# Six score blocks per visit to the half-high array tiles, and one pool of six PSUM banks, in a fused attention and MLP kernel

## The chip, the cores and the metric

The kernel runs on one core of one Trainium2 chip. The metric is the device time of one execution in microseconds, of the slowest core, which here is the only one. Each kernel is run several times, beside runs of the kernel before on the same chip. All runs quoted here were classed as fast. A ratio always compares with the kernel before in the same session. Engines are named as in the profile: PE does matrix products, PEld is its weight load, ACT is the scalar engine, DVE the vector engine, POOL the general one, SP the one that issues most of the DMA transposes here. A name with a q behind it (SPq) is that engine's sequencer.

## The reference

```python
# u, v: (8, 3008, 256)   z: (8, 3008, 64)   w_in: (256, 2048)   w_out: (2048, 256)
scores = (1 / 3008) * (z @ z.transpose(0, 2, 1))      # per batch: 3008 x 3008, symmetric
attn   = np.maximum(scores, 0.0) ** 2
x      = u * (attn @ v)                               # 24064 tokens of 256
h      = x @ w_in
out    = (h * np.cos(h)) @ w_out
```

The score matrix is symmetric. The kernel computes it in blocks of 512 x 512, and takes a block below the diagonal as the transpose of the one above it.

## The kernel before

The kernel is a list of pieces of work with a time in "units". Each piece is a few matmuls and what follows them on ACT and DVE. The pieces are sorted by their time, and each engine is given its own in that order. A column of 512 tokens of one batch takes eight units; a batch has six columns. There are five kinds of matmul:

- scores (S): 64 rows deep (`dqk` = 64), so that two run side by side in the upper and the lower half of the array (in the trace they start 3 ns apart, and a pair takes the 216 ns of one);
- attention times v (av): 128 rows, 512 columns;
- the last half block of attention (`av_half`): 64 rows, in two halves of the array;
- h = x w_in: 128 rows, 512 columns;
- y = g w_out: 128 rows, 256 columns.

A visit is an uninterrupted run of 64-row matmuls between 128-row ones. Before the change, a visit is one group of four score blocks, on four of the five banks of the pool `ps_w`. (A bank is here one tile of the program's PSUM pools, into which its matmuls write; it holds one block of 128 x 512.) y has a bank of its own, in which two token blocks are interleaved.

```python
gpool = pool("g", 6)
...
ps_w = psum("ps_w", 5)
ps_acc = psum("ps_acc", NDH)
ps_y = psum("ps_y", 1)
...
def direct(b, c, R):                  # batch 0, columns 0-2: all blocks computed
    return b == 0 and c <= 2          # at once, none waits for a transpose
...
def s_diagonal(b, c, also):
    ...                               # 512, 384, 256 and 128 columns: the upper part only
    for k0 in range(0, K, 2):
        ...                           # Relu on ACT, square on DVE, then, for three of four:
                nc.sync.dma_start_transpose(
                    t[:, k + 1:, k, :],
                    t[:, k, k + 1:, :].rearrange("p s w -> p (s w)"))

def s_group(b, c, R, also=None):
    if R == c and (b, c) > (0, 3):
        return s_diagonal(b, c, also)
    ...                               # four matmuls of 512 columns, Relu, squares
    if R > c and not direct(b, R, c):
        tt = tpool.tile([P, K, K, P], FP16, name="tt")
        turned[(b, c, R)] = tt
        nc.sync.dma_start_transpose(  # the mirrored block, 512 x 512
            tt.rearrange("p s k w -> p (s k) w"),
            t.rearrange("p s k w -> p (s k w)"))
```

A diagonal group (R == c) has three small transposes of its own, except where it is computed whole: in columns 0 to 3 of batch 0.

## Time and profile before

The median of the first three runs was 1257.65 us (1257.07 to 1258.25).

| what | value | read from |
|---|---|---|
| PE busy | 1245.4 of 1255.9 us | first part of the page |
| ACT, DVE busy | 68%, 63% | first part of the page |
| a 512-column matmul, start to start | 215.8 ns | start times of PE's matmuls |
| a 256-column matmul | 109.2 ns | the same |
| a visit of four score blocks | 633 ns: 2 x 216 + 201 | the same |
| PE's waits after 62 us | under 1 us | the same, and the view of waits |

First, the page of the kernel before: its span; busy time, share of the span and instructions for PE, DVE and ACT; the clock that PE was granted in 40 slices, in tenths; and the chain of work that ended last.

```profile
span 1255.9 us, 20306 instructions
...
PE 1245.4 (99%) x7533; PEld 672.0 (54%) x7533; DVE 791.0 (63%) x1389; ACT 853.9 (68%) x1516; POOL 145.8 (12%) x201
...
PEclk9999999999999999999999999999999999999999
...
PE 97%; ACT 1%; DVE 1%; issue 0%; DMA 0%; ACTq 0%
```

PE is the chain. Matmuls overlap in this profile (each lasts 379 ns and starts 216 after the one before), so the busy share alone does not tell how full PE is. Start times do.

Second, the timeline of the kernel before around one visit: start, length, engine, line, operation, operands. L308 is av, L249 scores, L365 y.

```profile
510.50 0.38 PE L308 MATMUL acc<-a,v_2_70 128*128 128x512 f16 x1
...
510.81 0.61 PE L249 MATMUL w<-zT_64 64*128 64x512 f16 x4
...
511.34 0.61 PE L365 MATMUL yp<-w_out_73,g 128*128 128x256 f16 x4
```

From the last av to the first score there are 312 ns where 216 are due, and from the last score (at 511.04) to the first y 308. This is what a visit costs beyond its matmuls: 96 ns going in and 93 coming out, and with the small offsets between the pairs 201 ns for a visit.

### The profile page before, as it was taken

How to read it: one execution, taken by the hardware profiler on the slowest of the kernel's cores; microseconds unless marked ns; L12 is line 12 of the kernel's file. 1: busy time of each engine (PE TensorE's matmuls, PEld its weight loads, DVE VectorE, ACT ScalarE, POOL GpSimd, SP SyncE). 2: the span in 40 equal slices, each digit the busy share in tenths (PEclk: the TensorE clock that was granted, in tenths of full speed). 3: DMA queues.
4: the chain of work that ended last, by engine and by line, in shares of the span. 5: the costliest groups of instructions: out<-in, count | busy, mean ns of one | idle time of the engine just before them, and what ended most of it. 6: DMA issues, size and time to landing. Idle time of an engine off the chain costs nothing.

```text
span 1255.9 us, 20306 instructions
## 1 busy us (share of the span) xinstructions
PE 1245.4 (99%) x7533; PEld 672.0 (54%) x7533; DVE 791.0 (63%) x1389; ACT 853.9 (68%) x1516; POOL 145.8 (12%) x201
## 2 busy tenths in 40 slices
PE   8999999999999999999999999999999999999998
PEld 3355555555555555555555555555555555555556
DVE  7766666666666666666666666666666656666555
ACT  6766776676766767666676666766767767766646
POOL 3311001110011100111001110011100111000000
PEclk9999999999999999999999999999999999999999
DMA  9999467875778956787667975679766797565311
GB/s 166 157 190 133 90 113 115 140 123 93 118 110 140 121 99 116 111 141 114 109 110 109 147 114 106 113 106 147 116 105 113 110 139 126 100 110 102 67 34 43
DMA packets 484179, 144.84 MB, mean 115 GB/s; under 512 B 432368, under 2 KB 484080, under 8 KB 484080
## 3 DMA queue, kind: packets, MB, share of 16 engines
q1 hardware_dynamic: 356448, 88.73, 42.5%
q0 software_dynamic: 100400, 29.77, 23.9%
q10 hardware_dynamic: 27232, 25.06, 7.0%
q8 instruction: 59, 0.97, 0.3%
q14 instruction: 40, 0.33, 0.1%
HBM read 60.29 MB, written 24.64 MB: 68 GB/s over the span
## 4 chain that ended last, share of the span: by engine, by line
PE 97%; ACT 1%; DVE 1%; issue 0%; DMA 0%; ACTq 0%
PE acc L308 37%; PE yp L365 26%; PE w L341 26%; PE w L249 5%; PE w L219 1%; PE acc L282 1%; PE w L365 1%; ACT rt L261 0%; DMA x<-in_z_dram 0%; DVE a L264 0%; DVE g L348 0%; ACT zT_63 L197 0%; DVE x L329 0%; PE w L192 0%; ACT L345 0%
## 5 line engine op out<-in xcount | busy, mean ns | idle before, releaser
L341 PE MATMUL w<-x,w_in_72 128*128 128x512 f16 x1504 | 446.2, 379 | 0.2 <-DVE g L348 0.2
L365 PE MATMUL yp<-w_out_73,g 128*128 128x256 f16 x2944 | 442.3, 273 | 0.4 <-ACT ob L373 0.4
L365 PEld LDWEIGHTS <-g 128*128 128x128 f16 x3008 | 285.2, 98 | 207.5 <-issue 41.5
L261 ACT ACTIVATE rt<-w 128x512 f16<-128x512 f32 x489 | 252.8, 604 | 102.6 <-PE w L249 102.6
L264 DVE TENSOR_TENSOR a<-rt 128x1024 f16<-128x1024 f16 x254 | 174.0, 690 | 154.8 <-ACT rt L261 150.1
L341 PEld LDWEIGHTS <-w_in_72 128*128 128x128 f16 x1504 | 147.0, 98 | 22.3 <-issue 3.4
L90 POOL DMA_DIRECT2D ust_62<-in_u_dram x64 | 45.2, 711 | 372.0 <-PE w L249 371.4
L229 ACT ACTIVATE rt<-w 128x512 f16<-128x512 f32 (+3 forms) x176 | 62.7, 443 | 32.7 <-PE w L219 32.7
L308 PE MATMUL acc<-a,v_2_70 128*128 128x512 f16 x304 | 80.0, 379 | 0.0
L308 PE MATMUL acc<-a,v_2_67 128*128 128x512 f16 x304 | 79.7, 379 | 0.0
L308 PE MATMUL acc<-tt,v_0_68 128*128 128x512 f16 (+1 forms) x288 | 73.6, 373 | 0.0
L90 POOL DMA_DIRECT2D ust_61<-in_u_dram x48 | 36.1, 758 | 306.9 <-PE acc L308 297.3
L329 DVE TENSOR_TENSOR x<-acc,ut 128x64 f16<-128x64 f32 (+7 forms) x178 | 69.6, 431 | 1.3 <-PE acc L308 1.3
L308 PE MATMUL acc<-tt,v_0_65 128*128 128x512 f16 (+1 forms) x264 | 67.4, 373 | 0.0
L230 DVE TENSOR_TENSOR a<-rt 128x512 f16<-128x512 f16 (+3 forms) x176 | 48.2, 322 | 27.7 <-ACT rt L229 27.7
L308 PEld LDWEIGHTS <-v_0_65 128*128 128x128 f16 x384 | 36.6, 98 | 47.3 <-issue 5.9
L308 PEld LDWEIGHTS <-v_1_66 128*128 128x128 f16 x384 | 36.6, 98 | 47.3 <-issue 6.6
L308 PEld LDWEIGHTS <-v_0_68 128*128 128x128 f16 x384 | 36.9, 98 | 45.7 <-issue 3.4
L308 PEld LDWEIGHTS <-v_1_69 128*128 128x128 f16 x384 | 36.9, 98 | 44.9 <-issue 2.6
L308 PE MATMUL acc<-a,v_1_66 128*128 128x512 f16 x224 | 59.3, 379 | 0.8 <-DVE x L329 0.7
L308 PE MATMUL acc<-a,v_1_69 128*128 128x512 f16 x224 | 59.4, 379 | 0.0
L373 ACT ACTIVATE ob<-yp 128x512 f32<-128x512 f32 x92 | 56.0, 608 | 1.2 <-PE yp L365 1.2
(1557 smaller groups left out, 1507.6 us busy)
## 6 DMA issues: line engine op xcount, KB each, us to landing
out_dram<-ob ACTq DMA_DIRECT2D x94, 256.0 KB, 3.5
ust_61<-in_u_dram POOLq DMA_DIRECT2D x48, 128.0 KB, 5.9
ust_62<-in_u_dram POOLq DMA_DIRECT2D x32, 128.0 KB, 3.4
a<-a SPq DMA_TRANSPOSE x132, 3.0
v_0_65<-in_v_dram POOLq DMA_DIRECT2D x4, 512.0 KB, 8.1
v_1_66<-in_v_dram POOLq DMA_DIRECT2D x4, 512.0 KB, 6.2
v_0_68<-in_v_dram POOLq DMA_DIRECT2D x4, 512.0 KB, 8.5
v_1_69<-in_v_dram POOLq DMA_DIRECT2D x4, 512.0 KB, 6.9
```

The lines of the kernel that those rows point to most:

```text
L90: hold(nc.gpsimd.dma_start(dst, src))
L219: chain(nc.tensor.matmul(sps[k][:, k * P:], zt[h, j0 + k, :], zt[h, j0 + k:j0 + K, :].rearrange("p j w -> p (j w)"), start=True, stop=True))
L229: nc.scalar.activation(rt[:, i, k * P:], sps[k][:, k * P:], AF.Relu)
L230: nc.vector.tensor_tensor(t[:, k, k:, :].rearrange("p s w -> p (s w)"), rt[:, i, k * P:], rt[:, i, k * P:], ALU.mult)
L249: chain(nc.tensor.matmul(sps[k], zt[h, R * K + k + 1 - lo, :], zt[h, j0:j0 + K, :].rearrange("p j w -> p (j w)"), start=True, stop=True))
L261: nc.scalar.activation(rt[:, i, :], sps[k0 + i], AF.Relu)
L264: nc.vector.tensor_tensor(tv, rv, rv, ALU.mult)
L308: chain(nc.tensor.matmul(acc[nh][:, 0:wn], vs[b % 2][j // G][:, j % G, nh * P:(nh + 1) * P], a, start=(n == 0), stop=(n == NJ - 2)))
L329: nc.vector.tensor_tensor(x[:, nh, :], acc[nh][:, o:o + n], ut[:, nh, o:o + n], ALU.mult)
L341: chain(nc.tensor.matmul(hp, w_in16[:, k, ft * P:(ft + 1) * P], x[:, k, :], start=(k == 0), stop=(k == NDH - 1)))
L365: chain(nc.tensor.matmul(ys[m][:, ts % YP, :], gs[(m, ft // FG)][:, ft % FG, ts * P:(ts + 1) * P], w_out16[:, ft, :], start=(n % (YP * NFT ...
L373: nc.scalar.activation(ob, ys[m], AF.Copy, bias=0.0, scale=inv_s2)
```

## The change

The intent is fewer visits: six score blocks in each, on all six banks of one pool, which y shares. To free y's bank, y is accumulated one token block at a time. The schedule is laid out in steps of two units (four h tiles and 16 y matmuls, then 12 av with a visit among them). v is kept in a ring of four tiles in place of six, which pays for two more g tiles.

```diff
-    vs = [[kpool.tile([P, G, D], FP16, name=f"v{i}_{g}") for g in range(NG)]
-          for i in range(2)]
+    vring = [kpool.tile([P, G, D], FP16, name=f"v{i}") for i in range(NG + 1)]
+    vs = lambda b, g: vring[(b * NG + g) % (NG + 1)]
...
-    gpool = pool("g", 6)
+    gpool = pool("g", 8)
...
-    ps_w = psum("ps_w", 5)
+    ps_w = psum("ps_w", 6)
     ps_acc = psum("ps_acc", NDH)
-    ps_y = psum("ps_y", 1)
...
-    def s_group(b, c, R, also=None):
-        if R == c and (b, c) > (0, 3):
-            return s_diagonal(b, c, also)
...
+    def s_matmuls(b, c, R, p):                 # a pair: two of a group's four blocks
...
+        diagonal = R == c and not direct(b, c, R)
...
+    def s_visit(pairs, also=None):
+        done = [(pair, s_matmuls(*pair)) for pair in pairs]
         if also is not None:
             also()
+        for pair, banks in done:
+            s_squares(*pair, banks)
...
+    NV = 3                                      # pairs in a visit
...
+        for i in range(0, len(pairs), NV):
+            some = [pr for pr in pairs[i:i + NV] if not direct(*pr[:3])]
+            t = b * span - lead + span * i / len(pairs)
+            if some:
+                scores.append((2 * math.floor(t / 2) + 1.2, some))
...
+                for q, f in enumerate(av_chunks(b, c, [4, 2] * (U // 2))):
+                    at(t + q // 2 * 2 + (1.4 if q % 2 else 1.0), 2, f)
```

`(b, c) > (0, 3)` became `not direct(b, c, R)`. The two differ for one group only, the diagonal one of batch 0, column 3.

More of the change, by code (lines that the diff above doesn't have):

```diff
@@ L117, in load_v @@
     def load_v(b, g):
-        t = vs[b % 2][g]
+        t = vs(b, g)
         n, full, rest = rows(v, b, g)
@@ L208, in direct, with s_squares @@
         return b == 0 and c <= 2
-    def s_diagonal(b, c, also):
+    halves = {}
+    def s_matmuls(b, c, R, p):
         zt = zT[b % 2]
-        t = apool.tile([P, K, K, P], FP16, name="a")
-        sps = [ps_w.tile([P, CW], FP32, name="w") for k in range(K)]
-        for k in (0, 1, 3, 2):
-            lo = 1 if k in (1, 2) else 0
+        banks = {}
+        diagonal = R == c and not direct(b, c, R)
+        for k in ((0, 1), (3, 2) if diagonal else (2, 3))[p]:
+            s0 = k if diagonal else 0
+            lo = 1 if k in ((1, 2) if diagonal else (1, 3)) else 0
             h = slice(lo * dqk, (lo + 1) * dqk)
             j0 = c * K + 1 - lo
+            sp = ps_w.tile([P, CW], FP32, name="w")
             chain(nc.tensor.matmul(
-                sps[k][:, k * P:], zt[h, j0 + k, :],
-                zt[h, j0 + k:j0 + K, :].rearrange("p j w -> p (j w)"),
+                sp[:, s0 * P:], zt[h, R * K + k + 1 - lo, :],
+                zt[h, j0 + s0:j0 + K, :].rearrange("p j w -> p (j w)"),
                 start=True, stop=True))
-        if also is not None:
-            also()
-        for k0 in range(0, K, 2):
-            rt = rpool.tile([P, 2, CW], FP16, name="rt")
+            banks[k] = sp
+        return banks
+    def s_squares(b, c, R, p, banks):
+        if p == 0:
+            halves[(b, c, R)] = apool.tile([P, K, K, P], FP16, name="a")
+        t = halves[(b, c, R)]
+        diagonal = R == c and not direct(b, c, R)
+        rt = rpool.tile([P, 2, CW], FP16, name="rt")
+        if diagonal:
             for i in range(2):
-                k = k0 + i
-                nc.scalar.activation(rt[:, i, k * P:], sps[k][:, k * P:], AF.Relu)
+                k = 2 * p + i
+                nc.scalar.activation(rt[:, i, k * P:], banks[k][:, k * P:], AF.Relu)
                 nc.vector.tensor_tensor(
@@ L236, in s_diagonal @@
                         t[:, k, k + 1:, :].rearrange("p s w -> p (s w)"))
-        fresh[(b, c, c)] = [t[:, k, :, :] for k in range(K)]
-    def s_group(b, c, R, also=None):
-        if R == c and (b, c) > (0, 3):
-            return s_diagonal(b, c, also)
-        zt = zT[b % 2]
-        t = apool.tile([P, K, K, P], FP16, name="a")
-        sps = [ps_w.tile([P, CW], FP32, name="w") for k in range(K)]
-        for k in range(K):
-            lo = k % 2
-            h = slice(lo * dqk, (lo + 1) * dqk)
-            j0 = c * K + 1 - lo
-            chain(nc.tensor.matmul(
-                sps[k], zt[h, R * K + k + 1 - lo, :],
-                zt[h, j0:j0 + K, :].rearrange("p j w -> p (j w)"),
-                start=True, stop=True))
+            if p == 1:
+                fresh[(b, c, R)] = [t[:, k, :, :] for k in range(K)]
@@ new lines, in s_squares @@
+            return
+        for i in range(2):
+            k = 2 * p + i
+            if direct(b, c, R) and (k == 3 or c == R == 0 and i):
+                nc.vector.tensor_scalar_max(rt[:, i, :], banks[k], 0.0)
+            else:
+                nc.scalar.activation(rt[:, i, :], banks[k], AF.Relu)
+        rv = rt.rearrange("p k (s w) -> p k s w", s=K)
+        nc.vector.tensor_tensor(
+            t.rearrange("p s k w -> p k s w")[:, 2 * p:2 * p + 2], rv, rv, ALU.mult)
+        if p == 1:
+            fresh[(b, c, R)] = [t[:, :, k, :] for k in range(K)]
+            if R > c and not direct(b, R, c):
+                tt = tpool.tile([P, K, K, P], FP16, name="tt")
+                turned[(b, c, R)] = tt
+                nc.sync.dma_start_transpose(
+                    tt.rearrange("p s k w -> p (s k) w"),
+                    t.rearrange("p s k w -> p (s k w)"))
@@ L253, in s_group @@
+    def s_visit(pairs, also=None):
+        done = [(pair, s_matmuls(*pair)) for pair in pairs]
         if also is not None:
             also()
-        for k0 in range(0, K, 2):
-            rt = rpool.tile([P, 2, CW], FP16, name="rt")
-            for i in range(2):
-                if direct(b, c, R) and (k0 + i == 3 or c == R == 0 and i):
-                    nc.vector.tensor_scalar_max(rt[:, i, :], sps[k0 + i], 0.0)
-                else:
-                    nc.scalar.activation(rt[:, i, :], sps[k0 + i], AF.Relu)
-            tv = t.rearrange("p s k w -> p k s w")[:, k0:k0 + 2]
-            rv = rt.rearrange("p k (s w) -> p k s w", s=K)
-            nc.vector.tensor_tensor(tv, rv, rv, ALU.mult)
@@ L265, in s_group @@
-        fresh[(b, c, R)] = [t[:, :, k, :] for k in range(K)]
-        if R > c and not direct(b, R, c):
-            tt = tpool.tile([P, K, K, P], FP16, name="tt")
-            turned[(b, c, R)] = tt
-            nc.sync.dma_start_transpose(
-                tt.rearrange("p s k w -> p (s k) w"),
-                t.rearrange("p s k w -> p (s k w)"))
+        for pair, banks in done:
+            s_squares(*pair, banks)
     xs = {}
@@ L283, in av_half, with av_chunks @@
                 accs[(b, c)][nh],
-                vs[b % 2][NG - 1][h, G - 1, nh * P:(nh + 1) * P],
+                vs(b, NG - 1)[h, G - 1, nh * P:(nh + 1) * P],
                 a[h], start=False, stop=False))
-    def av_quanta(b, c):
+    def av_chunks(b, c, sizes):
         w = min(CW, S - c * CW)
-        per = -(-NJ // U)
         order = [(c + i) % NC * K + k for i in range(NC) for k in range(K)]
@@ L298, in moving, with chunk @@
             return w, tt[:, k, 0:w]
-        def quantum(q):
-            if q == 0:
+        def chunk(n0, n1):
+            if n0 == 0:
                 accs[(b, c)] = [ps_acc.tile([P, CW], FP32, name="acc") for nh in range(NDH)]
@@ L304, in quantum @@
             for nh in range(NDH):
-                for n in range(q * per, min(NJ - 1, (q + 1) * per)):
+                for n in range(n0, n1):
                     j = order[n]
@@ L309, in quantum @@
                         acc[nh][:, 0:wn],
-                        vs[b % 2][j // G][:, j % G, nh * P:(nh + 1) * P], a,
+                        vs(b, j // G)[:, j % G, nh * P:(nh + 1) * P], a,
                         start=(n == 0), stop=(n == NJ - 2)))
-            if q == U - 1:
+            if n1 == NJ - 1:
                 finish()
@@ L330, in finish @@
                         x[:, nh, :], acc[nh][:, o:o + n], ut[:, nh, o:o + n], ALU.mult)
-        return [lambda q=q: quantum(q) for q in range(U)]
+        ends = [min(sum(sizes[:i]), NJ - 1) for i in range(len(sizes) + 1)]
+        return [lambda i=i: chunk(ends[i], ends[i + 1]) for i in range(len(sizes))]
     gs = {}
@@ L350, with y_quantum @@
     ys = {}
+    obs = {}
     NTS = TW // P
-    YP = 2
-    def y_quantum(m, q):
-        per = NFT * NTS // (2 * U)
-        for n in range(q * per, (q + 1) * per):
-            ts, ft = n // (YP * NFT) * YP + n % YP, n % (YP * NFT) // YP
-            if n % (YP * NFT) == 0:
-                if m >= NT - 2 and n:
-                    ys[m] = ps_w.tile([P, CW], FP32, name="w").rearrange(
-                        "p (t d) -> p t d", d=D)
-                else:
-                    ys[m] = ps_y.tile([P, YP, D], FP32, name="yp")
-            chain(nc.tensor.matmul(
-                ys[m][:, ts % YP, :],
-                gs[(m, ft // FG)][:, ft % FG, ts * P:(ts + 1) * P],
-                w_out16[:, ft, :],
-                start=(n % (YP * NFT) == 0),
-                stop=(n % (YP * NFT) == YP * NFT - 1)))
-            if (n + 1) % (YP * NFT) == 0:
-                ob = opool.tile([P, YP, D], FP32, name="ob")
-                nc.scalar.activation(ob, ys[m], AF.Copy, bias=0.0, scale=inv_s2)
-                r0 = m * TW + (ts - YP + 1) * P
+    def y_quantum(m, ts, f4):
+        if f4 == 0:
+            ys[m] = ps_w.tile([P, CW], FP32, name="w")
+        for ft in range(f4 * FG, (f4 + 1) * FG):
+            chain(nc.tensor.matmul(
+                ys[m][:, 0:D], gs[(m, f4)][:, ft % FG, ts * P:(ts + 1) * P],
+                w_out16[:, ft, :], start=(ft == 0), stop=(ft == NFT - 1)))
+        if f4 == NFT // FG - 1:
+            if ts % 2 == 0:
+                obs[m] = opool.tile([P, 2, D], FP32, name="ob")
+            i = ts % 2
+            nc.scalar.activation(
+                obs[m][:, i, :], ys[m][:, 0:D], AF.Copy, bias=0.0, scale=inv_s2)
+            i0 = i if m == NT - 1 else 0
+            if i or m == NT - 1:
+                r0 = m * TW + (ts - i + i0) * P
                 nc.scalar.dma_start(
-                    out[r0:r0 + YP * P, :].rearrange("(ts p) d -> p ts d", p=P), ob)
+                    out[r0:r0 + (i + 1 - i0) * P, :].rearrange("(ts p) d -> p ts d", p=P),
+                    obs[m][:, i0:i + 1, :])
     events = []
@@ L388 @@
     lead = 1.75 * U
+    NV = 3
     scores = []
+    when = {}
     for b in range(B):
-        for i, (c, R) in enumerate(groups):
-            if not direct(b, c, R):
-                t = math.floor(b * span - lead + span * i / len(groups))
-                scores.append((t - 0.1 if t % U == U - 1 else t + 0.9, b, c, R))
+        pairs = [(b, c, R, p) for c, R in groups for p in range(2)]
+        for i in range(0, len(pairs), NV):
[3 more added lines that the diff above has]
+                scores.append((2 * math.floor(t / 2) + 1.2, some))
         for c in range(NC):
@@ L398 @@
                 for i in range(NC):
-                    scores.append((c * U + 4 * i / 3 - 3.1, b, c, (c + i) % NC))
+                    R = (c + i) % NC
+                    scores.append((c * U + 4 * i / 3 - 3.1, [(b, c, R, 0), (b, c, R, 1)]))
+    for t, some in scores:
+        for pr in some:
+            when[pr[:3]] = max(t, when.get(pr[:3], t))
     also = {}
@@ L403 @@
             t = b * span + c * U
-            ready = 1.5 + max(ts for ts, bb, cc, R in scores
-                              if (bb, cc, R) == (b, c, NC - 1))
-            room = [sc for sc in scores if max(ready, t + 0.6) < sc[0] < t + U - 1.07]
+            ready = 1.5 + when[(b, c, NC - 1)]
+            first, last = (0.6, 6.93) if direct(b, c, c) else (1.0, 7.3)
+            room = [i for i, sc in enumerate(scores)
+                    if max(ready, t + first) < sc[0] < t + last and i not in also]
             if room:
-                also[min(room)] = lambda b=b, c=c: av_half(b, c)
+                also[min(room, key=lambda i: scores[i][0])] = lambda b=b, c=c: av_half(b, c)
             else:
-                at(t + U - 1.07, 3, lambda b=b, c=c: av_half(b, c))
-            for q, f in enumerate(av_quanta(b, c)):
-                at(t + q + (0.5 if q < U - 1 else -0.05), 2, f)
-    for sc in scores:
-        at(sc[0], 3, lambda sc=sc: s_group(*sc[1:], also=also.get(sc)))
+                at(t + last, 3, lambda b=b, c=c: av_half(b, c))
+            if direct(b, c, c):
+                for q, f in enumerate(av_chunks(b, c, [3] * U)):
+                    at(t + q + (0.5 if q < U - 1 else -0.05), 2, f)
+            else:
+                for q, f in enumerate(av_chunks(b, c, [4, 2] * (U // 2))):
+                    at(t + q // 2 * 2 + (1.4 if q % 2 else 1.0), 2, f)
+    for i, (t, some) in enumerate(scores):
+        at(t, 3, lambda i=i, some=some: s_visit(some, also=also.get(i)))
     for m in range(NT):
         b, i = divmod((m + 1) * TW - 1, S)
-        th = max(20 + m * U, (b * NC + i // CW + 1) * U + 1)
+        th = max(20 + m * U, (b * NC + i // CW + 1) * U + 2)
         for ft in range(NFT):
-            at(th + ft // 2 + (0.3 if ft % 2 else 0.1), 1,
-               lambda m=m, ft=ft: h_quantum(m, ft))
-        for q in range(2 * U):
-            at(th + U - 2 + q // 2 + (0.2 if q % 2 else 0.0), 4,
-               lambda m=m, q=q: y_quantum(m, q))
+            at(th + ft // 4 * 2 + ft % 4 * 0.2, 1, lambda m=m, ft=ft: h_quantum(m, ft))
+        for ts in range(NTS):
+            for f4 in range(NFT // FG):
+                at(th + U + 2 * ts + 0.1 + 0.2 * f4, 4,
+                   lambda m=m, ts=ts, f4=f4: y_quantum(m, ts, f4))
     for b in range(B):
@@ L442 @@
             for g in range(NG):
-                at(t + (0.75 * g - 2.5) * U, 0, lambda b=b, g=g: load_v(b, g))
+                at(t + (-1.5, -0.4, -0.1)[g] * U, 0, lambda b=b, g=g: load_v(b, g))
         for c in range(3 if b == 0 else 0, NC):
```

## The prediction

The sum: 10.2 + 0.15 + 0.7 + 0.3, about 11.4 us off, and 1 us on.

> **What bounds the kernel.** TensorE. The page's first part has PE busy 1245.4 of 1255.9 us, ACT 68%, DVE 63%; the chain of waits that ended last is 97% PE. From the start times of its matmuls, a 512-column one takes 215.8 ns of the array, a 256-column one 109.2, and after the first 62 us PE loses under 1 us to waits. So only work taken off PE's own stream counts. The granted clock is 1.0.
>
> **What a visit costs.** The score matmuls (64 rows, in two tiles of the array) and the half-block matmuls of attention interrupt the 128-row stream. Going in, the gap is 311.6 ns where 215.8 is due; coming out, 308.5. A visit of four score blocks takes 633 ns, two pairs at 216 and 201 of switching; one of two half-block matmuls 418, one pair and 202. [...]
>
> **What the change does.** The instruction order shows the same 7533 matmuls before and after. Runs of 64-row matmuls fall from 172 to 121 (57 of six full blocks, 45 with a diagonal): 51 x 0.201 = 10.2 us, all on the critical path. One more diagonal group is done at its smaller size (0.15 us). y by token block in the common pool lets the last 64 y matmuls start while the last g is made, where PE waits 0.7 us before; the last eviction and store are half as large (0.3 us). Total: about 11.4 us.
>
> **What it adds.** 188 y evictions of 256 columns replace 94 of 512. Start to start on ACT, back to back, a 512-column Relu takes 477 ns, a Sin 569, an eviction of half the size about 290 (estimate, from the 256-column Relu's 263): roughly +10 us of ACT, off the path. A six-block visit fills all six banks. A two-unit period with a visit is 6.9 us of PE (8 h matmuls 1.73, 16 y 1.75, 12 attention 2.59, visit 0.85); ACT needs 6 x 0.477 + 4 x 0.569 + 0.29 = 5.4 us, DVE about 3 x 0.61 + 4 x 0.60 = 4.2, with the x evictions at most 5.8. So each catches up even where two periods in a row have visits (four times a batch). After a visit the next h needs the first bank some 1.2 to 1.6 us after the scores began; Relu gives it back after about 1.0 and the others each 0.48 later, while PE asks for one after 0.44, then each 0.87. That is close where the last attention piece has two matmuls, but should cost 0.1 us or less a time: 1 us in all. The v ring has some 19 us for loads that land in 6 to 9: no cost.
>
> **Prediction.** 1257.65 - 11.4 + 1 = about 1247 us, range 1243.5 to 1252. Faster by over 2%: 1%; within 2%: 97%; slower: 2%.
>
> **What would show it.** In the matmul start times: 121 visits, 849 ns for six blocks, 1065 with a half block, entry and exit still near 96 and 93 ns; waits after 62 us still near 1 us.
>
> **What would make it wrong.** Waits of h, y or the third pair of scores on Relu or g (bank turnaround longer than I think), seen as waits of PE on ACT or DVE all through the batches; v late at batch boundaries; more waiting in the first 100 us, where h runs without y; an extra cost when consecutive y matmuls add into the same 256 columns.

## The result, and the profile after

The changed kernel took 1258.69 us (median of 6, 1255.98 to 1261.33), beside 1257.68 for the kernel before. The ratio is 1.0008, with a 95% interval of 0.9992 to 1.0023: the same. A ratio here is the mean time of one kernel's fast runs over the mean of the other's fast runs of the same rounds, so it is not quite the ratio of the medians. About 11 us were predicted and none came.

The page of the changed kernel, the lines that answer to those of before, and one group of matmuls (its last numbers are the idle time before them and what ended it):

```profile
span 1256.7 us, 20414 instructions
...
PE 1238.2 (99%) x7533; PEld 680.4 (54%) x7533; DVE 782.0 (62%) x1391; ACT 845.6 (67%) x1610; POOL 146.0 (12%) x201
...
PEclk9979999999999999999999999999999999999999
...
PE 96%; DMA 2%; DVE 1%; ACT 0%; SPq 0%; issue 0%; DVEq 0%
...
L310 PE MATMUL acc<-a,v_66 128*128 128x512 f16 x312 | 81.3, 385 | 7.7 <-DMA a<-a 6.4
```

PE is busy 7.2 us less in a span of the same length. One slice of the clock reads 7, DMA has entered the chain with 2%, and one group of av matmuls waited 6.4 us for the DMA that turns a score block inside its own tile (a<-a).

The time can be cut at two matmuls that both kernels have. I use the start of the 97th h matmul (in the first batch) and of the 1441st (near the end of the last).

| us | before | after | difference |
|---|---|---|---|
| start to the 97th h | 125.23 | 134.88 | +9.65 |
| 97th to 1441st h | 1088.76 | 1078.82 | -9.94 |
| 1441st h to the end | 41.94 | 42.96 | +1.02 |

So the gain is there, all through the batches, and the first 135 us give it back. The first and the last row also hold a shift of order: before the 97th h the kernel before has done 148 y matmuls and the changed one 128, and the other 20 (2.2 us) come after the 1441st h instead. For the same y work, the start lost 11.8 us and the end gained 1.2.

The steady part is as predicted. Between the two matmuls there are 143 visits before and 96 after, and they take 93.8 and 83.2 us. The timeline of the changed kernel around a visit (L223 is scores):

```profile
633.77 1.89 PE L310 MATMUL acc<-a,v_67 128*128 128x512 f16 x8
635.59 0.82 PE L223 MATMUL w<-zT_63 64*128 64x512 f16 x6
636.34 0.60 PE L310 MATMUL acc<-a,v_67 128*128 128x512 f16 x2
```

From the last of the eight av to the next av there are 850 ns beyond its own 216: three pairs at 216 and again 201 for the visit itself.

The loss is here, in the timeline of PE in the changed kernel (L344 is h, L310 av; the bracket gives idle time and what ended it):

```profile
63.07 3.30 PE L344 MATMUL w<-x,w_in_70 128*128 128x512 f16 x8 [0.75 <-DVE g L351]
66.21 0.38 PE L310 MATMUL acc<-a,v_66 128*128 128x512 f16 x1
71.65 0.59 PE L310 MATMUL acc<-a,v_66 128*128 128x512 f16 x1 [5.06 <-DMA a<-a]
72.92 0.59 PE L310 MATMUL acc<-a,v_66 128*128 128x512 f16 x1 [0.68 <-DMA a<-a]
74.19 2.29 PE L310 MATMUL acc<-a,v_66 128*128 128x512 f16 x5 [0.68 <-DMA a<-a]
```

And this is SP's DMA queue in the same kernel (start, time in the sequencer, what it issues):

```profile
40.92 28.22 SPq L265 DMA_TRANSPOSE tt<-a  x5
69.31 3.74 SPq L245 DMA_TRANSPOSE a<-a  x3
73.10 4.19 SPq L265 DMA_TRANSPOSE tt<-a  x2
```

At 66.21 PE reaches column 3 of batch 0. The first matmul uses the part of the diagonal group that DVE wrote; the next three need the parts that the three small transposes write. DVE had finished the squares at 54.55. The three were issued only at 69.31, 70.58 and 71.86, because five long transposes (128 x 2048 elements each) held SP for 28 us, 5.6 each in the mean (3.7 to 7.6), while the three took 1.2 each. They landed at 71.61, 72.87 and 74.14, and PE went on 0.04 to 0.05 us after each. From the start of the first of these four matmuls to the start of the fourth took 7.98 us, where 0.65 (3 x 216 ns) are due.

In the kernel before, SP had the same long transposes, but nothing of column 3's first matmuls was among them:

```profile
41.13 29.83 SPq L269 DMA_TRANSPOSE tt<-a  x6
71.13 1.76 SPq L150 DMA_TRANSPOSE ut<-ust_62  x1
```

The clock adds to it. In the changed kernel 20 matmuls of 512 columns between 58 and 80 us start some 427 ns apart instead of 216, which is another 4.1 us; the view by windows gives a granted clock of 0.50 from 62.6 to 65.9 us and from 69.4 to 79.6. What makes the clock fall was not shown; what can be read is what came before. Seven of the 20 (1.4 us) begin at 63.07, before the long wait, so that wait did not cause them: they follow 4 us with small waits (1.33, 0.23, 0.23 and 0.75 us), after DVE had stood 4.79 us (to 59.33) for a long transpose. The other 13 (2.7 us) follow the long wait.

### The profile page after: what moved, and what is told of

It is laid out like the page before. It is cut to its first block, busy times and chain, and to the rows that moved or that the text cites. A ratio compares the mean times of both kernels' runs of the same rounds, so it can differ in the third digit from the quotient of the medians.

```text
span 1256.7 us, 20414 instructions
## 1 busy us (share of the span) xinstructions
PE 1238.2 (99%) x7533; PEld 680.4 (54%) x7533; DVE 782.0 (62%) x1391; ACT 845.6 (67%) x1610; POOL 146.0 (12%) x201
## 4 chain that ended last, share of the span: by engine, by line
PE 96%; DMA 2%; DVE 1%; ACT 0%; SPq 0%; issue 0%; DVEq 0%
PE acc L310 37%; PE w L361 26%; PE w L344 26%; PE w L223 6%; DMA tt<-a 1%; PE acc L285 1%; DMA ut<-ust_62 1%; DVE g L351 0%; DMA x<-in_z_dram 0%; SPq L245 0%; DMA a<-a 0%; ACT zT_63 L196 0%; DVE a L258 0%; DVE x L331 0%; ACT rt L256 0%
## 5 line engine op out<-in xcount | busy, mean ns | idle before, releaser
L344 PE MATMUL w<-x,w_in_70 128*128 128x512 f16 x1504 | 447.9, 381 | 0.8 <-DVE g L351 0.8
L361 PE MATMUL w<-w_out_71,g 128*128 128x256 f16 x3008 | 448.6, 273 | 0.0
L361 PEld LDWEIGHTS <-g 128*128 128x128 f16 x3008 | 294.2, 98 | 191.6 <-issue 1.4
L344 PEld LDWEIGHTS <-w_in_70 128*128 128x128 f16 x1504 | 147.6, 98 | 61.1 <-issue 7.3
L310 PEld LDWEIGHTS <-v_66 128*128 128x128 f16 x552 | 52.1, 98 | 68.4 <-issue 21.6
L310 PE MATMUL acc<-a,v_66 128*128 128x512 f16 x312 | 81.3, 385 | 7.7 <-DMA a<-a 6.4
L310 PE MATMUL acc<-a,v_65 128*128 128x512 f16 x336 | 85.8, 380 | 0.0
L310 PEld LDWEIGHTS <-v_67 128*128 128x128 f16 x552 | 52.1, 98 | 59.3 <-issue 12.3
L310 PEld LDWEIGHTS <-v_65 128*128 128x128 f16 x552 | 51.6, 98 | 59.8 <-issue 12.2
L310 PEld LDWEIGHTS <-v_68 128*128 128x128 f16 x552 | 51.9, 98 | 57.7 <-issue 10.9
L310 PE MATMUL acc<-a,v_67 128*128 128x512 f16 x312 | 80.0, 383 | 0.0
L310 PE MATMUL acc<-a,v_68 128*128 128x512 f16 x312 | 79.2, 379 | 0.0
L368 ACT ACTIVATE ob<-w 128x256 f32<-128x256 f32 x188 | 73.0, 388 | 5.3 <-PE w L361 5.3
L310 PE MATMUL acc<-tt,v_68 128*128 128x512 f16 (+1 forms) x240 | 62.2, 371 | 0.0
L310 PE MATMUL acc<-tt,v_67 128*128 128x512 f16 (+1 forms) x240 | 62.1, 371 | 0.0
```

The costliest lines, as they stand in the source:

```text
L310: chain(nc.tensor.matmul(acc[nh][:, 0:wn], vs(b, j // G)[:, j % G, nh * P:(nh + 1) * P], a, start=(n == 0), stop=(n == NJ - 2)))
L344: chain(nc.tensor.matmul(hp, w_in16[:, k, ft * P:(ft + 1) * P], x[:, k, :], start=(k == 0), stop=(k == NDH - 1)))
L361: chain(nc.tensor.matmul(ys[m][:, 0:D], gs[(m, f4)][:, ft % FG, ts * P:(ts + 1) * P], w_out16[:, ft, :], start=(ft == 0), stop=(ft == NFT ...
L368: nc.scalar.activation(obs[m][:, i, :], ys[m][:, 0:D], AF.Copy, bias=0.0, scale=inv_s2)
```

## The experiments

Two theories of the loss stood at this point. Theory A: the diagonal group of batch 0, column 3, now needs transposes that stand behind the long ones. Theory B: the loss comes from what was changed on purpose, that is, visits that fill every bank, bursts of h at the start, and a clock that falls because of them.

### e1: that one group whole again

```diff
-        diagonal = R == c and not direct(b, c, R)
+        diagonal = R == c and (b, c) > (0, 3)
```

(in both places of the changed kernel)

> The changed kernel with one group, the diagonal one of batch 0, column 3, computed whole as in the kernel before (no transposes of its own). Theory A (its three transposes stand behind the long ones in SP's DMA queue, PE waits 5.06 + 0.68 + 0.68 us and then runs 5 us at half clock): about 10 us less than the changed kernel, 1248 us; no wait of PE on a<-a. Theory B (the loss in the first 80 us comes from the longer bursts of h and the six-bank visits, not from this group): 1257 to 1259, the wait moves to another releaser.

Measured: 1248.35 us (median of 6, 1246.67 to 1250.74), ratio to before 0.9915 (0.9895 to 0.9935). That is 10.3 us less than the changed kernel's median; by the ratios to the kernel before (1.0008 and 0.9915) it is 0.93%, or 11.7 us. It was run at another time. The result is correct.

The view of who waited for whom, for PE, in the changed kernel and then in e1 (in us: total, times, longest):

```profile
PE acc L310 <- DMA a<-a: 6.4, 3, 5.1
PE w L223 <- DVE g L351: 3.0, 6, 1.3
PE acc L310 <- DVE x L331: 1.3, 1, 1.3
```

```profile
PE acc L310 <- DVE x L331: 2.9, 1, 2.9
PE w L223 <- ACT zT L196: 1.6, 2, 1.1
PE w L470 <- DVE rt L467: 1.2, 1, 1.2
PE w L223 <- DVE g L351: 1.2, 4, 0.5
```

The wait on a<-a is gone, and column 3 starts at 65.97 us and runs on at full clock, 216 ns from start to start:

```profile
65.97 2.75 PE L310 MATMUL acc<-a,v 128*128 128x512 f16 x12
```

That is only 0.24 us sooner than in the changed kernel, so the half clock before the long wait does not set the two apart. What does is the wait (7.3 us) and the half clock after it (2.7). The 97th h starts at 124.69 us (134.88 in the changed kernel, 125.23 in the kernel before), and the stretch from there to the 1441st is 1078.82 us, the same as in the changed kernel. Theory A holds, and theory B doesn't: the six-bank visits and the bursts of h are all still there.

### e2: the same condition in the kernel before

```diff
-        if R == c and (b, c) > (0, 3):
+        if R == c and not direct(b, c, R):
```

> The kernel before with that one group done as a diagonal one with three transposes, nothing else changed. Theory A: the same stall appears in the kernel before, 6 to 12 us slower than it, 1264 to 1270 us, with PE waiting on a<-a near 60 to 72 us. Theory B: no difference above 1 us.

Measured: 1275.96 us (median of 4), ratio 1.0128 (1.0103 to 1.0152), about 17 us slower than the kernel before. This is more than I had expected. PE gets to column 3 sooner than in the changed kernel (63.77 us against 66.21) and the three transposes are issued later (72.54 against 69.31), so the first wait is 10.75 us against 5.06; and the granted clock is 0.50 from 68 to 84.9 us. The timeline of e2:

```profile
63.77 0.38 PE L308 MATMUL acc<-a,v 128*128 128x512 f16 x1 [0.31 <-DVE x L329]
74.89 0.59 PE L308 MATMUL acc<-a,v 128*128 128x512 f16 x1 [10.75 <-DMA a<-a]
76.15 1.87 PE L308 MATMUL acc<-a,v 128*128 128x512 f16 x4 [0.67 <-DMA a<-a]
```

One condition, for one group, without any of the rest of the change, makes the loss.

### e3: four blocks per visit

```diff
-    NV = 3
+    NV = 2
```

(on top of e1)

> e1 with four score blocks per visit (NV = 2) in place of six: 172 runs of 64-row matmuls in place of 121, everything else as in e1. If a visit's switching costs 0.201 us wherever it stands: e1 + 10.2 us. If the gain of fewer visits is taken by waits on banks (rival): e1 within 3 us.

Measured: 1254.48 us (median of 6, 1252.2 to 1256.53), ratio 0.9963 (0.9941 to 0.9986), so 6.1 us slower than e1. In the steady stretch between the 97th and the 1441st h it takes 1087.00 us, 8.2 more than e1. There it has 143 visits against 96. They take 92.5 us against 83.2, 9.3 more: 0.198 for each of the 47. That is the predicted price. Some 1.1 us come back in the rest of the stretch, which is neither visits nor the nominal time of the other matmuls (1.44 us in e3, 2.58 in e1): e1 has small waits after its fuller visits. The start went 2.4 us better in this profile (97th h at 122.24; the trace has 6.8 us of waits of PE before it, against 8.3 in e1), so the whole kernel shows less than the 10.2 expected. I had expected the total, and it fell between the two theories; the stretch settles it.

### e5: the three transposes from ACT's queue

```diff
-                    nc.sync.dma_start_transpose(
+                    (nc.scalar if b == 0 and c == 3 else nc.sync).dma_start_transpose(
                         t[:, k + 1:, k, :],
```

(on top of the changed kernel)

> The changed kernel with the three transposes of that group issued from ACT's queue, so that they do not stand behind the long ones of SP's queue. If the place in the queue is the cause: they land by about 60 us, no wait of PE on them, about 8 to 10 us less than the changed kernel. If the transposes are slow in themselves under the load of DMA at that time: PE still waits for them for several us, gain under 4 us.

Measured: 1268.96 us (median of 4), ratio 1.008, 10 us slower than the changed kernel. This does not test what it was meant to test. It was run at another time. The view of waits on ACT:

```profile
ACT rt L256 <- DMA a<-a: 20.9, 1, 20.9
```

The first of the three was issued at 75.38, just after the last long transpose of SP had landed at 75.08. In the trace, ACT's sequencer waits before it for eight semaphores, from 57.12 us on. These waits stand in the program as it was built from the edit: the eight semaphores are those of the last eight transposes issued by SP before. (What happens without them was not run.) So the wait did not go away, and it now also stood in front of ACT's Relus. In this run another queue was no way around.

### e6 and e7: the long transposes taken away

To take the queue away without touching the three, the nine long transposes of columns 0 to 2 of batch 0 are replaced by zeros from POOL. The results are wrong (relative error 0.12). e6 is the changed kernel with that edit, e7 is e1 with it.

```diff
                 turned[(b, c, R)] = tt
-                nc.sync.dma_start_transpose(...)
+                if direct(b, c, R):
+                    nc.gpsimd.memset(tt, 0.0)
+                else:
+                    nc.sync.dma_start_transpose(...)
```

> The changed kernel, wrong result on purpose: in batch 0 the nine mirrored blocks of columns 0 to 2 are filled with zeros by POOL in place of the nine long transposes that stand in SP's DMA queue ahead of the diagonal group's three. The three themselves stay. If standing behind the long ones is the cause: they land by about 58 us, no wait of PE on a<-a, and the time is within 2 us of e7_full03_no_queue. If the three are slow by themselves: PE still waits for them and the time is 5 us or more above e7.

> The control to e6: the same zeros (wrong result on purpose), with the group computed whole. It also shows what the nine long transposes cost in all: 1242 to 1247 us, since the waits on u's transposes and on buffers near 40 and 60 us should go too.

Measured: e6 1245.93 us (median of 4, 1243.49 to 1247.21), e7 1244.29 us (1243.63 to 1245.58). They were run at other times. SP's queue and PE in e6:

```profile
20.74 9.50 SPq L150 DMA_TRANSPOSE ut<-ust  x2
53.21 3.74 SPq L245 DMA_TRANSPOSE a<-a  x3
```

```profile
59.52 1.90 PE L347 MATMUL w<-x,w_in 128*128 128x512 f16 x8
61.26 2.75 PE L313 MATMUL acc<-a,v 128*128 128x512 f16 x12
```

The three transposes take the same 3.74 us of the sequencer as in the changed kernel, but at 53.21 in place of 69.31. The last landed at 59.23 (I had expected about 58), and column 3 starts at 61.26 without a wait. Together with the changed kernel and e1 this makes a square (medians):

| | long transposes ahead | none ahead |
|---|---|---|
| three transposes of the group | 1258.69 | 1245.93 |
| group computed whole | 1248.35 | 1244.29 |

With the queue, the three cost 10.3 us; without it, 1.6, which is no more than the scatter of these runs. By the ratios to the kernel before in the same session (1.0008, 0.9915; 0.9888, 0.9878) it is 11.7 us and 1.3. It is their place behind the long transposes, not the three in themselves. The edit also takes the nine transposes out of the DMA's work altogether, so the two columns may differ by more than the queue, but both rows of the second have that alike.

### e8 and e9: two attempts to improve the start

e8 is e1 with a Sin as the first activation, so that ACT loads Sin's table at the beginning. e9 is e8 with u's transposes of columns 1 and 2 placed earlier in SP's queue.

```diff
-        nc.scalar.activation(dummy, pihalf, AF.Relu)
+        nc.scalar.activation(dummy, pihalf, AF.Sin)
```

```diff
-            at(t + c * U + (1 if b or c not in (1, 2) else -3 * c), 0, lambda b=b, c=c: turn_u(b, c))
+            at(t + c * U + (1 if b or c not in (1, 2) else (-6.5, -8)[c - 1]), 0, lambda b=b, c=c: turn_u(b, c))
```

> e1 with the dummy activation at the start a Sin in place of a Relu, so that the table that Sin needs is loaded at 1 us and not at 52 us, where 1.28 us of it stood in front of the first Sin while PE waited 1.5 us on banks: 1 to 1.5 us less than e1, about 1247; no second table load in the trace. If a Relu makes the first table be loaded again, no gain.

> e8 with u's transposes of columns 1 and 2 of batch 0 placed ahead of the long ones in SP's queue: the wait of PE near 39 us (1.4 us in the changed kernel's trace, 3.0 in e1's) goes: 1.5 to 3 us less than e8, about 1244 to 1245. If the long transposes only move the wait to later: within 1 us of e8.

Measured: e8 1249.41 us (median of 6, 1248.11 to 1253.47), e9 1248.28 us (1244.03 to 1254.75). They were run on another chip. Neither differs from e1 beyond the scatter, and e9's 1.1 us below e8 doesn't tell its two expectations apart. In e8 the second table load of 1.28 us (at 52.30 in e1) is gone and the one at 1.28 us is left, and the waits of PE's scores between 50 and 57 us fell from 0.95 us to 0.35 (by the idle times of the timeline), but the wait for u near 39 us was longer in that profile (3.7 us against 3.0), so nothing shows in the total. In e9 the wait for u's transpose went, but DVE then waited for a buffer that a long transpose was still reading, and PE still waited near 40 us. The timeline of e9:

```profile
39.16 1.29 DVE L258 TENSOR_TENSOR a<-rt 128x1024 f16<-128x1024 f16 x2 [1.56 <-DMA tt<-a]
...
41.11 1.24 PE L310 MATMUL acc<-a,v 128*128 128x512 f16 x5 [1.47 <-DVE x L331]
```

e7, which has no long transposes there, is about 4 us below e1 (medians of two sessions): that is what they still cost e1 at the start. What else the start could give was not tried. Whether e8's table load is worth anything by itself stays open; it is below the scatter of the start.

The simplest of the best correct versions is e1, 0.9915 of the time of the kernel before (e9, at 0.9910, does not differ from it).

## Why the prediction was wrong

- "What bounds the kernel" was right. PE is the chain, and what was taken off its stream came off the time, in the steady part.
- "What a visit costs" was right: 633 ns before and 850 after for a visit of four and of six blocks, 201 of it for the visit itself, and about 0.198 us for each visit in e3 against e1.
- "51 x 0.201 = 10.2 us" was right in kind and size. In the measured stretch 47 visits fewer took 10.6 us less. About 1.1 us of that is not switching: seven diagonal visits took 647 ns before, where eight others took 486, and the changed kernel's have the shorter form.
- The 1.0 us for the end (0.7 and 0.3) was near: for the same y work, the stretch after the 1441st h is 1.2 us shorter.
- "1 us in all" for waits on banks was near. What is left of the stretch after the visits and the nominal matmul times (and so holds their rounding too) is 2.58 us after and 1.94 before.
- "The v ring ... no cost" is supported by the trace only: in the changed kernel's view of waits none of PE's, down to 0.4 us, is on a v load. No run changed the ring by itself.
- **The step that failed is "One more diagonal group is done at its smaller size (0.15 us)".** I saw that the condition had changed, counted the array time it saves, and stopped there. A diagonal group also brings three DMA transposes, and column 3 of batch 0 starts with exactly that group. In SP's queue they stood behind five long ones that took 28 us. The term that I put at -0.15 us measured +10.3 (e1 against the changed kernel; 11.7 by the ratios), and +17 in the kernel before (e2).
- The list of what could go wrong named "more waiting in the first 100 us", but for another cause, "where h runs without y". That was not the 10 us: e1 has the same bursts of h. The extra cost it named for consecutive y matmuls that add into the same 256 columns did not come: from one to the next are 109 ns in the changed kernel, as before. But the start of e1 does cost something. It reaches the 97th h 0.5 us before the kernel before does, with 20 y matmuls and 4 visits (3.0 us together) fewer done by then, so it is about 2.5 us behind. Its longest wait is 2.95 us for x at 42.18, which DVE could make only when u's transpose had landed, followed by four matmuls at half clock. This is one profile, and no run separates its causes.

With that one term put right, the prediction stands: e1's 1248.35 us are 1.35 above the 1247 predicted, and inside its range. That it comes so close is in part luck: the 1.1 us of the diagonal visits and the 2.5 us of the start were both not in the sum, and have opposite signs.

## What to carry to other kernels

When a change rewrites a condition, ask for each case that moves from one side to the other what it now waits for, and not only how much work it has. A DMA that is short by itself takes its place in its queue's order (here 1.2 us of SP's sequencer, issued 14.8 us after DVE had finished the squares): look at the queue's timeline at the moment of issue, above all in the first microseconds (here DMA moved 165 GB/s from 36 to 80 us, and 113 from there to 1235). And when a change shows no difference, cut both traces at a matmul that they share: here a gain and a loss of 11 to 12 us in different places had cancelled. Count also what each kernel has done by then: at the 97th h the two differed by 20 y matmuls.
